# Attention in two passes: pass 1 of the next unit is issued between the key tiles of pass 2 of the current one

## The chip, the core and the metric

The kernel runs on one core of a Trainium2 chip. A core has a matrix engine (TensorE, PE in the profile; PEld is its weight load), a vector engine (VectorE, DVE), a scalar engine (ScalarE, ACT), GpSimd (POOL) and SyncE (SP); each works through its own queue in order, and they meet through semaphores. Transfers go through DMA queues that SP, ACT (here SPq and ACTq) and POOL issue. SBUF is the working memory; PSUM takes the results of matmuls and has 8 banks of 2 KiB per partition. The metric is the device time of one execution in microseconds (us).

## The reference

Two layers work on 2048 tokens of width 1024 and are mixed by a gate. The change is in layer A, softmax attention with 32 heads of 32:

```python
def _A_ref(x, wqkv, wo):
    qkv = (x @ wqkv).reshape(B, S, 3, H, Dh).transpose(2, 0, 3, 1, 4)
    q, k, v = (qkv[0], qkv[1], qkv[2])
    scale = Dh ** (-0.5)
    scores = jnp.einsum('bhqd,bhkd->bhqk', q, k) * scale
    p = _softmax(scores, axis=-1)
    o = jnp.einsum('bhqk,bhkd->bhqd', p, v)
    return o.transpose(0, 2, 1, 3).reshape(B, S, D) @ wo
...
g = _sigmoid((x * gate_w).sum(-1, keepdims=True))
return g * a + (1 - g) * b
```

Layer B (`b`) is a recurrence over 64 segments of 32 tokens; each needs the memory that the one before wrote.

## The kernel before

The program has three stages, one after the other: the projections of layer A (with the transposes of x and the gate), attention with its output projection (`phaseA_attn`), and the recurrence of layer B (`phase2_recurrence`), which adds A's part at the end. Only `phaseA_attn` is touched.

Attention runs over 4 query chunks (`qc`) of 512 queries and, in each, 8 groups (`g`) of 4 heads: 32 units. For a unit, four `KTm` tiles (a head's keys, 128 x 2048, other heads' rows zero) and four `Qaug` tiles (128 x 512 queries) are loaded from `ka_s` and `qa_s` by SP's and ACT's queues (L454, L455), into one of two sets of buffers, and POOL clears one row of each `Qaug` (L456). A unit has two passes:

- Pass 1 finds each query's largest score. For 4 heads, 4 query tiles and 4 key chunks, 64 in all, PE makes a score tile `sq`, 128 queries x 512 keys (L462), and DVE takes its maximum into `mp` (L464). Then DVE folds `mp` into `negm` (L466), 16 small transposes turn it into rows in `nr_ps` (L470), and ACT and DVE in turn (`ev`, L56 and L58) copy one row into each `Qaug` (L473). KTm has ones there, so pass 2 gets the maximum subtracted by its matmul.
- Pass 2 goes over 16 key tiles. In each, for every head, PE makes `st`, 128 keys x 512 queries (L479), and ACT takes the exponent into `p_sb` (L482); then a group of four matmuls per head adds its product with the values to `o_ps` (L486), whose last column is the sum. At the end DVE takes reciprocals, multiplies by the gate `gcol` and scales into `OA` (L493 to L499).

After 8 units the chunk is projected: for 4 query tiles, 8 transposes of `OA` into `trA` (L506), a copy `oat`, and 16 matmuls with `wo_sb` into `psA3` (L513), which are copied to `stageA` and stored (L516).

PSUM is shared out by pools: `pq` has 3 banks for everything tagged `sq` (`sq`, `nr_ps`, `trA`, `psA3`), `pt` 3 for `st`, `po` 2 for `o_ps`. The order on each engine is not that of the text: the framework's scheduler places instructions by priority (earlier in the text first) and by when buffers and inputs are free. So pass 1 of a unit already starts, in the order, during pass 2 of the unit before.

## Time and profile before

| | |
|---|---|
| median of 6 runs | 4604.24 us (4595.59 to 4608.38) |
| the profiled execution: its time, its span | 4595.59 us, 4593.8 us |
| busy share of the span: PE, DVE, ACT | 87%, 48%, 34% |
| first maximum of attention to its last `negm` | 249.63 us to 1945.43 us |
| mean granted clock of TensorE | 0.917 |

The span goes from the first to the last instruction of the profiled execution. Shares over the whole span mix stages: attention takes some 1755 us of it and the recurrence the last 2590 us, which keeps the DMA engines busy and DVE and ACT not. In attention the clock row of the profile stands at 7 to 8 tenths, in the recurrence at 9. A time in the rows below is counted from the span's start. A line such as L58 or L56 is the copy helper's; the tile names tell what was copied. Busy time of an engine that overlaps its own next instruction (the mean of one is then longer than the spacing) counts once.

### The profile page before, as it was taken

Reading aid. Unit: us, or ns where it says so; the run is one execution under the profiler, and the core shown is the slowest. Engines: PE = TensorE matmul, PEld = TensorE weight load, DVE = VectorE, ACT = ScalarE, POOL = GpSimd, SP = SyncE. Lnnn points to the kernel's source line nnn. Section 1 sums busy time; section 2 is a strip of 40 time slices with the busy share of each in tenths; the row PEclk is TensorE's granted clock in tenths of the full one; section 3 lists DMA queues with packets and bytes.
Section 4 is the critical chain, followed back from the end, with each engine's and each line's share of the span. In section 5 each row is a group of like instructions: output and inputs, shape, how many; then the busy total and the mean of one; then the engine's idle time right before and its main releaser. Section 6 shows DMA issues by size and latency. Waiting matters only on the chain.

```text
span 4593.8 us, 127170 instructions
## 1 busy us (share of the span) xinstructions
PE 4005.2 (87%) x57232; PEld 2042.9 (44%) x57476; DVE 2216.5 (48%) x3778; ACT 1576.4 (34%) x3049; POOL 285.5 (6%) x524
## 2 busy tenths in 40 slices
PE   6978889888898898859898888888888888888888
...
DMA packets 235026, 918.69 MB, mean 200 GB/s; under 512 B 23016, under 2 KB 39400, under 8 KB 158832
## 3 DMA queue, kind: packets, MB, share of 16 engines
...
q14 instruction: 96, 0.79, 0.1%
...
## 4 chain that ended last, share of the span: by engine, by line
PE 55%; ACT 14%; DVE 14%; DMA 12%; issue 4%; POOL 0%; ACTq 0%; SPq 0%; POOLq 0%; DVEq 0%
PE pjm L259 11%; PE wps L359 11%; DVE mp L464 11%; DMA wp<-in_B_Wk_dram 10%; PE pjx L259 9%; ACT p_sb L482 9%; PE st L479 6%; PE sq L462 4%; PE o_ps L486 3%; PE tr L282 2%; PE ps L402 2%; PE ops L340 1%; ACT QmT L56 1%; PE psA L513 1%; PE ops L343 1%
## 5 line engine op out<-in xcount | busy, mean ns | idle before, releaser
L464 DVE TENSOR_REDUCE mp<-sq 128x1 f32<-128x512 f32 x2048 | 1287.8, 683 | 171.7 <-PE sq L462 169.7
L482 ACT ACTIVATE p_sb<-st 128x512 bf16<-128x512 f32 x2048 | 1019.0, 722 | 46.8 <-PE st L479 44.0
L462 PE MATMUL sq<-KTm,Qaug 128*128 128x512 bf16 x2020 | 891.6, 448 | 111.4 <-DVE mp L464 73.3
L479 PE MATMUL st<-Qaug,KTm 128*128 128x512 bf16 x1856 | 705.9, 393 | 20.3 <-ACT Qaug L56 13.7
L486 PEld LDWEIGHTS <-p_sb 128*128 128x128 bf16 x8192 | 433.2, 97 | 478.3 <-ACT p_sb L482 298.8
L259 PEld LDWEIGHTS <-memT 128*32 128x32 bf16 x12288 | 360.3, 97 | 475.2 <-issue 178.1
L486 PE MATMUL o_ps<-V_A,p_sb 128*128 128x33 bf16 x8192 | 524.7, 180 | 20.3 <-ACT p_sb L482 13.9
L259 PEld LDWEIGHTS <-xs 128*32 128x32 bf16 x12288 | 386.5, 97 | 285.4 <-issue 5.9
L259 PE MATMUL pjm<-wp,memT 128*32 128x512 bf16 x4608 | 362.6, 382 | 104.9 <-DMA wp<-in_B_Wk_dram 103.5
L462 PEld LDWEIGHTS <-Qaug 128*128 128x128 bf16 x2048 | 196.9, 99 | 429.8 <-issue 402.2
L259 PE MATMUL pjx<-wp,xs 128*32 128x512 bf16 x4608 | 362.5, 381 | 0.2 <-issue 0.2
L359 PEld LDWEIGHTS <-oT 128*32 128x32 bf16 x8128 | 229.2, 103 | 254.2 <-issue 67.4
L359 PE MATMUL wps<-res_o,oT 128*32 128x512 bf16 x5080 | 338.6, 405 | 0.0
L370 DVE SCALAR_TENSOR_TENSOR bo<-wps,omg,apt 64x512 bf16<-64x512 f32 x64 | 48.4, 757 | 505.1 <-ACT memn L56 498.7
L58 DVE CAST tm_km<-pjm 128x512 bf16<-128x512 f32 x64 | 44.3, 692 | 489.7 <-PE pjm L259 489.7
L58 DVE CAST tm_qm<-pjm 128x512 bf16<-128x512 f32 x64 | 44.3, 692 | 454.4 <-PE pjm L259 454.4
L259 PE MATMUL pjm<-res_q,memT 128*32 128x512 bf16 x2560 | 198.4, 382 | 66.5 <-DVE memT L58 52.0
L56 ACT COPY Qaug<-nr_ps 1x512 bf16<-1x512 bf16 x64 | 37.0, 578 | 584.6 <-PE nr_ps L470 569.8
L359 PE MATMUL wps<-wp,oT 128*32 128x512 bf16 x3048 | 226.8, 419 | 1.5 <-DMA wp<-in_B_Wo_dram 1.1
L56 ACT CAST tm_qm<-pjm 128x512 bf16<-128x512 f32 x64 | 37.5, 586 | 538.3 <-PE pjm L259 498.3
L259 PE MATMUL pjx<-res_v,xs 128*32 128x512 bf16 x2560 | 207.1, 379 | 0.3 <-issue 0.3
L259 PE MATMUL pjm<-res_v,memT 128*32 128x512 bf16 x2560 | 207.0, 380 | 0.0
...
## 6 DMA issues: line engine op xcount, KB each, us to landing
...
```

The source lines that it names most:

```text
L56: self.nc.scalar.copy(out=out, in_=in_)
L58: self.nc.vector.tensor_copy(out=out, in_=in_)
L259: nc.tensor.matmul(ps[u][32 * j:32 * j + 32, :], lhsT=lhs_of[w](kt), rhs=piece[:, c * 512:(c + 1) * 512], start=(kt == kts[0] and first), ...
L282: nc.tensor.transpose(tr[:, hp, :], tm[key][:, hp // 4, (hp % 4) * 128:(hp % 4 + 1) * 128], ident[:])
L359: nc.tensor.matmul(wps[32 * cg:32 * cg + 32, :], lhsT=lhsT, rhs=piece[:, hh, c * 512:(c + 1) * 512], start=(gi == 0 and hh == 0), stop=(gi ...
L370: nc.vector.scalar_tensor_tensor(out=bo[64:128], in0=wps[64:128, :], scalar=omg[64:128, s:s + 1], in1=apt[64:128], op0=ALU.mult, op1=ALU.add)
L402: nc.tensor.matmul(ps[:], lhsT=w_sb[:, kt, which * D + g * 128:which * D + (g + 1) * 128], rhs=xT[:, kt, ch * CH:(ch + 1) * CH], start=(kt ...
L462: nc.tensor.matmul(sq[:], lhsT=Qaug[b][hh][:, qt * 128:(qt + 1) * 128], rhs=KTm[b][hh][:, kc * KC:(kc + 1) * KC], start=True, stop=True)
L464: nc.vector.tensor_reduce(out=mp[:, hh, qt, kc:kc + 1], in_=sq[:], op=ALU.max, axis=AX.X)
L479: nc.tensor.matmul(st[:], lhsT=KTm[b][hh][:, kt * 128:(kt + 1) * 128], rhs=Qaug[b][hh][:], start=True, stop=True)
L482: nc.scalar.activation(out=p_sb[:], in_=st[:], func=ACT.Exp, scale=scale)
L486: nc.tensor.matmul(o_ps[qt // 2][:, qt % 2, hh, :], lhsT=pts[hh][:, qt * 128:(qt + 1) * 128], rhs=V_A[:, kt, 4 * g + hh, :], start=(kt == ...
```

## The change

The pass over units is written as a pipeline by hand. The first unit's pass 1 runs alone; then, in every key tile of a unit's pass 2, a sixteenth of the next unit's pass 1 follows (`pass1_slice`), and after the last key tile the next unit's maxima are finished (`pass1_finish`). Besides:

- A score tile `sq` is two banks, 128 x 1024, filled by two matmuls, and one DVE reduction takes the maximum of both: 32 reductions a unit. `mp` has every second column unused and is filled with -3e38 by POOL first.
- The pools `pq` and `pt` have two buffers each (`pq` now two of two banks).
- The four rows of `Qaug` are all copied by ACT.
- `o_ps` is copied to SBUF by DVE (`o_sb`), the reciprocals and the gate are applied there, and ACT scales into `OA`, 16 instructions of 128 x 32 a unit, with the factor as an operand of one value per partition.
- In the projection, `psA3` is two banks and is copied at once.

```diff
@@ -429,8 +429,8 @@
     cp = ctx.enter_context(tc.tile_pool(name="a2c", bufs=1))
     wk = ctx.enter_context(tc.tile_pool(name="a2w", bufs=2))
     ptp = ctx.enter_context(tc.tile_pool(name="a2pt", bufs=8))
-    pq = ctx.enter_context(tc.tile_pool(name="a2psq", bufs=3, space=PSUM))
-    pt = ctx.enter_context(tc.tile_pool(name="a2pst", bufs=3, space=PSUM))
+    pq = ctx.enter_context(tc.tile_pool(name="a2psq", bufs=2, space=PSUM))
+    pt = ctx.enter_context(tc.tile_pool(name="a2pst", bufs=2, space=PSUM))
     po = ctx.enter_context(tc.tile_pool(name="a2pso", bufs=1, space=PSUM))
 
     ident = cp.tile([128, 128], BF16, name="identA")
...
+    units = [(qc, g) for qc in range(NQC) for g in range(8)]
+    NU = len(units)
+    state = {}
+
+    def load(u):
+        qc, g = units[u]
+        b = u % 2
+        for hh in range(4):
+            dq[hh % 2].dma_start(KTm[b][hh][32 * hh:32 * hh + 32, :], ka_s[g, 32 * hh:32 * hh + 32, :])
+            dq[(hh + 1) % 2].dma_start(Qaug[b][hh][:], qa_s[g, :, qc * QC:(qc + 1) * QC])
+            nc.gpsimd.memset(Qaug[b][hh][RS[hh]:RS[hh] + 1, :], 0.0)
+        mp = wk.tile([128, 4, NQT, NKC], FP32, name="mp")
+        if KCG > 1:
+            nc.gpsimd.memset(mp[:], -3.0e38)
+        state[u] = dict(mp=mp)
+
+    KCG = 2 if NKC % 2 == 0 else 1
+    p1_items = [(hh, qt, kc) for hh in range(4) for qt in range(NQT) for kc in range(0, NKC, KCG)]
+
+    def pass1_slice(u, i, n):
+        b = u % 2
+        mp = state[u]["mp"]
+        lo, hi = i * len(p1_items) // n, (i + 1) * len(p1_items) // n
+        for hh, qt, kc in p1_items[lo:hi]:
+            sq = pq.tile([128, 2, 512], FP32, name="sq", tag="sq")
+            for i in range(KCG):
+                nc.tensor.matmul(sq[:, i, 0:KC], lhsT=Qaug[b][hh][:, qt * 128:(qt + 1) * 128],
+                                 rhs=KTm[b][hh][:, (kc + i) * KC:(kc + i + 1) * KC], start=True, stop=True)
+            nc.vector.tensor_reduce(out=mp[:, hh, qt, kc:kc + 1], in_=sq[:, 0:KCG, 0:KC], op=ALU.max, axis=AX.XY)
+
+    def pass1_finish(u):
+        b = u % 2
+        negm = wk.tile([128, 4, NQT], BF16, name="negm")
+        nc.vector.tensor_reduce(out=negm[:], in_=state[u]["mp"][:], op=ALU.max, axis=AX.X, negate=True)
+        nr_ps = pq.tile([128, 2 * 1024], BF16, name="nr_ps", tag="sq")
+        for hh in range(4):
+            for qt in range(NQT):
+                nc.tensor.transpose(nr_ps[RS[hh]:RS[hh] + 1, qt * 128:(qt + 1) * 128],
+                                    negm[:, hh, qt:qt + 1], ident[:], tile_position=(0, RS[hh]))
+        for hh in range(4):
+            nc.scalar.copy(out=Qaug[b][hh][RS[hh]:RS[hh] + 1, :], in_=nr_ps[RS[hh]:RS[hh] + 1, 0:QC])
+
+    def pass2_iter(u, kt):
+        qc, g = units[u]
+        b = u % 2
+        if kt == 0:
+            state[u]["o_ps"] = [po.tile([128, 2, 4, DA + 1], FP32, name=f"o_ps{i}") for i in range((NQT + 1) // 2)]
+        o_ps = state[u]["o_ps"]
+        pts = []
+        for hh in range(4):
+            st = pt.tile([128, QC], FP32, name="st")
+            nc.tensor.matmul(st[:], lhsT=KTm[b][hh][:, kt * 128:(kt + 1) * 128], rhs=Qaug[b][hh][:],
+                             start=True, stop=True)
+            p_sb = ptp.tile([128, QC], BF16, name="p_sb")
+            nc.scalar.activation(out=p_sb[:], in_=st[:], func=ACT.Exp, scale=scale)
+            pts.append(p_sb)
+        for hh in range(4):
+            for qt in range(NQT):
+                nc.tensor.matmul(o_ps[qt // 2][:, qt % 2, hh, :], lhsT=pts[hh][:, qt * 128:(qt + 1) * 128],
+                                 rhs=V_A[:, kt, 4 * g + hh, :],
+                                 start=(kt == 0 and hh == 0 and qt % 2 == 0), stop=(kt == nkt - 1),
+                                 skip_group_check=True)
+
+    def finalize(u, OA):
+        qc, g = units[u]
+        for i, ops_ps in enumerate(state[u]["o_ps"]):
+            nq = min(2, NQT - 2 * i)
+            ops = wk.tile([128, 2, 4, DA + 1], FP32, name=f"o_sb{i}")
+            nc.vector.tensor_copy(out=ops[:, 0:nq], in_=ops_ps[:, 0:nq])
+            rs = wk.tile([128, 2, 4], FP32, name="rs")
+            nc.vector.reciprocal(rs[:, 0:nq, :], ops[:, 0:nq, :, DA])
+            gq = gcol[:, qc * NQT + 2 * i:qc * NQT + 2 * i + nq]
+            nc.vector.tensor_tensor(out=rs[:, 0:nq, :], in0=rs[:, 0:nq, :],
+                                    in1=gq.unsqueeze(2).to_broadcast([128, nq, 4]), op=ALU.mult)
+            for q2 in range(nq):
                 for hh in range(4):
...
+                    nc.scalar.activation(out=OA[:, 2 * i + q2, 4 * g + hh, :], in_=ops[:, q2, hh, 0:DA],
+                                         func=ACT.Copy, scale=rs[:, q2, hh:hh + 1])
+        del state[u]
+
+    def out_proj(qc, OA):
         for qt in range(NQT):
             tt = qc * NQT + qt
...
+            tr = pq.tile([128, 2 * KT, 128], BF16, name="trA", tag="sq")
             OAf = OA[:, qt].rearrange("p h d -> p (h d)")
             for kt in range(KT):
                 nc.tensor.transpose(tr[:, kt, :], OAf[:, kt * 128:(kt + 1) * 128], ident[:])
             oat = wk.tile([128, KT, 128], BF16, name="oat")
...
+            ev(oat[:], tr[:, 0:KT, :])
             stage = wk.tile([128, D], FP32, name="stageA")
+            ps = pq.tile([128, 2, 512], FP32, name="psA3", tag="sq")
             for c in range(2):
...
                 for kt in range(KT):
...
+                    nc.tensor.matmul(ps[:, c, :], lhsT=oat[:, kt, :], rhs=wo_sb[:, kt, c * 512:(c + 1) * 512],
                                      start=(kt == 0), stop=(kt == KT - 1))
...
+            ev(stage[:].rearrange("p (c f) -> p c f", c=2), ps[:])
             nc.gpsimd.dma_start(ap_s[tt * 128:(tt + 1) * 128, :], stage[:])
+
+    load(0)
+    pass1_slice(0, 0, 1)
+    pass1_finish(0)
+    OA = None
+    for u in range(NU):
+        qc, g = units[u]
+        if g == 0:
+            OA = wk.tile([128, NQT, HA, DA], BF16, name="OA")
+        if u + 1 < NU:
+            load(u + 1)
+        for kt in range(nkt):
+            pass2_iter(u, kt)
+            if u + 1 < NU:
+                pass1_slice(u + 1, kt, nkt)
+        if u + 1 < NU:
+            pass1_finish(u + 1)
+        finalize(u, OA)
+        if g == 7:
+            out_proj(qc, OA)
```

The scheduler decides what this makes of the queues. On DVE, at the end of a unit (`L493` to `L499` before and `L516` to `L520` now are the unit's last scaling steps), stood:

```order
L464 TENSOR_REDUCE mp<-sq 128x1 x43
L493 RECIPROCAL rs<-o_ps_4739 128x8
L493 RECIPROCAL rs<-o_ps_4740 128x8
L497 TENSOR_SCALAR rs<-rs,gcol 128x4 x2
L499 TENSOR_TENSOR OA<-o_ps_4739,rs 128x128 x2
L497 TENSOR_SCALAR rs<-rs,gcol 128x4 x2
L499 TENSOR_TENSOR OA<-o_ps_4740,rs 128x128 x2
L464 TENSOR_REDUCE mp<-sq 128x1 x18
L466 TENSOR_REDUCE negm<-mp 128x16
```

and now stands:

```order
L476 TENSOR_REDUCE mp<-sq 128x1 x32
L481 TENSOR_REDUCE negm<-mp 128x16
L516 COPY o_sb_7274<-o_ps_6609 128x264
L516 COPY o_sb_7287<-o_ps_6610 128x264
L518 RECIPROCAL rs<-o_sb_7274 128x8
L518 RECIPROCAL rs<-o_sb_7287 128x8
L520 TENSOR_TENSOR rs<-rs,gcol 128x8 x2
```

The 18 maxima that stood behind the end of the current unit stand ahead of it, and each is twice as long.

On ACT, between two units' exponents (`p_sb`), stood:

```order
L482 ACTIVATE p_sb<-st 128x512 x63
L455 DMA Qaug_0_1470<-qa_s 128x512
L454 DMA KTm_1_1463<-ka_s 32x2048
L455 DMA Qaug_2_1472<-qa_s 128x512
L454 DMA KTm_3_1465<-ka_s 32x2048
L56 COPY Qaug_0_1474<-nr_ps 1x512
L482 ACTIVATE p_sb<-st 128x512
L56 COPY Qaug_2_1476<-nr_ps 1x512
L482 ACTIVATE p_sb<-st 128x512 x63
```

and now stands:

```order
L502 ACTIVATE p_sb<-st 128x512 x3
L456 DMA KTm_1_1467<-ka_s 32x2048
L488 COPY Qaug_0_1470<-nr_ps 1x512
L488 COPY Qaug_1_1471<-nr_ps 1x512
L488 COPY Qaug_2_1472<-nr_ps 1x512
L488 COPY Qaug_3_1473<-nr_ps 1x512
L524 ACTIVATE OA<-o_sb_8809,rs 128x32 x8
L524 ACTIVATE OA<-o_sb_8822,rs 128x32 x8
L457 DMA Qaug_2_1476<-qa_s 128x512
L456 DMA KTm_3_1469<-ka_s 32x2048
L502 ACTIVATE p_sb<-st 128x512 x61
```

Four copies, sixteen scalings and two of the loads' issues moved in between the exponents of one unit and the next.

On PE, at the first score tile of the unit after next (its `Qaug` and `KTm` take the buffers of the unit just ending), stood, behind all the `o_ps` groups and the small transposes:

```order
L462 LDWEIGHTS Qaug1_0_1474
L462 MATMUL sq_6786<-KTm1_0_1466,Qaug1_0_1474 128x512
L462 LDWEIGHTS Qaug1_0_1474
L462 MATMUL sq_6789<-KTm1_0_1466,Qaug1_0_1474 128x512
L479 LDWEIGHTS KTm0_0_1462
L479 MATMUL st_6249<-Qaug0_0_1470,KTm0_0_1462 128x512
```

and now stands, at one such place:

```order
L474 LDWEIGHTS Qaug1_0_1474
L474 MATMUL sq_11703<-KTm1_0_1466,Qaug1_0_1474 128x512
L474 LDWEIGHTS Qaug1_0_1474
L474 MATMUL sq_11703<-KTm1_0_1466,Qaug1_0_1474 128x512
L506 LDWEIGHTS p_sb_11580
L506 MATMUL o_ps0_10964<-V_A_69,p_sb_11580 128x33
```

The pair moved ahead of the last `o_ps` group of the ending unit.

## Rows read from the trace of the kernel before

**Rows 1.** Costliest groups: line, engine, tiles | busy us, mean ns | idle before, releaser.
```profile
L464 DVE TENSOR_REDUCE mp<-sq 128x1 f32<-128x512 f32 x2048 | 1287.8, 683 | 171.7 <-PE sq L462 169.7
L482 ACT ACTIVATE p_sb<-st 128x512 bf16<-128x512 f32 x2048 | 1019.0, 722 | 46.8 <-PE st L479 44.0
```

**Rows 2.** Busy us of each engine in stretches of one unit, then clock and DMA.
```profile
core 0: us, PE busy (x) PEld busy (x) DVE busy (x) ACT busy (x) POOL busy (x), PEclk, DMA share, GB/s
923.00:957.60 34.60, 33.54 (x360) 17.67 (x366) 30.24 (x48) 32.43 (x66) 0.00 (x0) 0.95 0.03 8
957.60:970.10 12.50, 8.77 (x17) 1.54 (x15) 12.47 (x30) 0.00 (x0) 2.07 (x4) 0.63 0.25 65
970.10:971.60 1.50, 1.17 (x17) 0.62 (x19) 0.24 (x2) 0.50 (x1) 0.00 (x0) 0.50 0.00 0
```

**Rows 3.** Timeline of DVE: start us, duration us, instruction, xcount [idle before <-releaser].
```profile
249.63 38.35 DVE L464 TENSOR_REDUCE mp<-sq 128x1 f32<-128x512 f32 x64 [16.94 <-PE sq L462]
288.02 0.22 DVE L466 TENSOR_REDUCE negm<-mp 128x16 bf16<-128x64 f32 x1
...
629.09 0.22 DVE L466 TENSOR_REDUCE negm<-mp 128x16 bf16<-128x64 f32 x1
...
726.46 0.22 DVE L466 TENSOR_REDUCE negm<-mp 128x16 bf16<-128x64 f32 x1
...
921.40 0.22 DVE L466 TENSOR_REDUCE negm<-mp 128x16 bf16<-128x64 f32 x1
...
959.17 10.84 DVE L464 TENSOR_REDUCE mp<-sq 128x1 f32<-128x512 f32 x18
970.05 0.22 DVE L466 TENSOR_REDUCE negm<-mp 128x16 bf16<-128x64 f32 x1
...
1945.43 0.22 DVE L466 TENSOR_REDUCE negm<-mp 128x16 bf16<-128x64 f32 x1
...
1980.97 0.28 DVE L493 RECIPROCAL rs<-o_ps 128x8 f32<-128x8 f32 x2 [31.61 <-PE o_ps L486]
```

**Rows 4.** Timeline of ACT around one unit boundary (ACTq: its DMA issues).
```profile
927.06 29.55 ACT L482 ACTIVATE p_sb<-st 128x512 bf16<-128x512 f32 x60 [0.85 <-PE st L479]
956.10 0.34 ACTq L455 DMA_DIRECT2D Qaug<-qa_s  x1
956.36 0.74 ACT L482 ACTIVATE p_sb<-st 128x512 bf16<-128x512 f32 x1
...
971.10 0.58 ACT L56 COPY Qaug<-nr_ps 1x512 bf16<-1x512 bf16 x1 [14.01 <-PE nr_ps L470]
972.38 0.60 ACT L482 ACTIVATE p_sb<-st 128x512 bf16<-128x512 f32 x1 [0.70 <-PE st L479]
```

**Rows 5.** Timeline of PE and PEld: in the output projection, at a boundary, in pass 2.
```profile
673.66 3.63 PE L513 MATMUL psA<-wo_sb,oat 128*128 128x512 bf16 x16 [0.79 <-DVE oat L58]
...
971.73 0.61 PE L479 MATMUL st<-Qaug,KTm 128*128 128x512 bf16 x1 [0.24 <-ACT Qaug L56]
...
973.03 0.29 PEld L486 LDWEIGHTS <-p_sb 128*128 128x128 bf16 x4 [0.65 <-ACT p_sb L482]
...
979.73 0.38 PE L479 MATMUL st<-Qaug,KTm 128*128 128x512 bf16 x1
979.94 0.38 PE L462 MATMUL sq<-KTm,Qaug 128*128 128x512 bf16 x1
980.16 0.26 PE L486 MATMUL o_ps<-V_A,p_sb 128*128 128x33 bf16 x4
980.26 0.66 PE L479 MATMUL st<-Qaug,KTm 128*128 128x512 bf16 x2
```

**Rows 6.** Timeline of POOL at the same boundary.
```profile
959.23 1.09 POOL L456 MEMSET Qaug<- 1x512 bf16 x2 [45.79 <-DMA Qaug<-qa_s]
```

**Rows 7.** Groups of ACT by line and shape, whole span: names, shapes | busy us, mean ns | idle before.
```profile
L56 ACT CAST oT<-ops 128x512 bf16<-128x512 f32 x128 | 75.0, 586 | 62.7 <-PE ops L343 62.7
L56 ACT COPY KTt<-tr 128x256 bf16<-128x256 bf16 x64 | 23.8, 373 | 14.4 <-PE tr L282 14.4
```

**Rows 8.** Who waited for whom, 925 to 957 us: us in total, times, longest.
```profile
PEld L486 <- ACT p_sb L482: 8.3, 32, 0.5
```

More of the change, by code (lines that the diff above doesn't have):

```diff
@@ L501, in phaseA_attn @@
+    def out_proj(qc, OA):
         for qt in range(NQT):
             tt = qc * NQT + qt
-            tr = pq.tile([128, KT, 128], BF16, name="trA", tag="sq")
+            tr = pq.tile([128, 2 * KT, 128], BF16, name="trA", tag="sq")
             OAf = OA[:, qt].rearrange("p h d -> p (h d)")
@@ L507, in phaseA_attn @@
             oat = wk.tile([128, KT, 128], BF16, name="oat")
-            ev(oat[:], tr[:])
+            ev(oat[:], tr[:, 0:KT, :])
             stage = wk.tile([128, D], FP32, name="stageA")
+            ps = pq.tile([128, 2, 512], FP32, name="psA3", tag="sq")
             for c in range(2):
-                ps = pq.tile([128, 512], FP32, name="psA3", tag="sq")
                 for kt in range(KT):
-                    nc.tensor.matmul(ps[:], lhsT=oat[:, kt, :], rhs=wo_sb[:, kt, c * 512:(c + 1) * 512],
+                    nc.tensor.matmul(ps[:, c, :], lhsT=oat[:, kt, :], rhs=wo_sb[:, kt, c * 512:(c + 1) * 512],
                                      start=(kt == 0), stop=(kt == KT - 1))
-                ev(stage[:, c * 512:(c + 1) * 512], ps[:])
+            ev(stage[:].rearrange("p (c f) -> p c f", c=2), ps[:])
             nc.gpsimd.dma_start(ap_s[tt * 128:(tt + 1) * 128, :], stage[:])
+    load(0)
[17 more added lines that the diff above has]
+            out_proj(qc, OA)
 @with_exitstack
```

53 lines of the change are left out of this document (removed).

## The prediction

> **What bounds the kernel now.** I read the costliest groups first, then the busy times of three stretches inside one unit, then the timelines of VectorE (DVE), ScalarE (ACT) and TensorE (PE) at one unit boundary. The costliest rows are the maximum `mp<-sq` on DVE, 2048 x 0.683 us alone, and the exponent `p_sb<-st` on ACT, 2048 x 0.722 us alone [rows 1]. Set in a row they come faster: 64 maxima in 38.35 us, 0.60 us each [rows 3], and 60 exponents in 29.55 us, 0.4925 us each [rows 4]. One unit has 64 of each, so 38.4 us of DVE and 31.5 us of ACT.
>
> The units are already overlapped: a unit's `negm` follows the last one's after 48.7 us (629.09 - 288.02 over 7 intervals, or 970.05 - 921.40) [rows 3], well under the 70 us of both passes. The overlap is partial. For 34.6 us both passes run and all three engines are nearly full (PE 33.5, ACT 32.4, DVE 30.2); then 12.5 us in which ACT does nothing, DVE is full and the clock falls to 0.63 [rows 2], while 18 maxima are worked off in 10.84 us [rows 3]; then 1.5 us of hand-over. At the change of a query chunk there is no overlap: the interval is 726.46 - 629.09 = 97.4 us [rows 3], since `trA` and `psA3` take the same PSUM buffers as `sq` and come first. So attention is 38.35 + 28 x 48.7 + 3 x 97.4 + 35.5 (the last pass 2, 1945.43 to 1980.97) plus the last output projection. The recurrence behind it is untouched and I give it no change.
>
> **The change part by part.** *Fewer, longer maxima.* 32 reductions over 1024 elements take the place of 64 over 512. No row shows 1024. From 64 elements (0.22 us [rows 3]) to 512 (0.683 [rows 1]) an element costs (0.683 - 0.22)/448 = 1.03 ns, so the longer one comes every 0.60 + 0.53 = 1.13 us. Below that is 2 x 0.53 = 1.06 (no fixed cost), above it 2 x 0.60 = 1.20 (nothing saved). 32 x 1.13 = 36.2 us a unit, 2.2 less than before. DVE also keeps about 1.7 us for `negm`, two copies of `o_ps` (264 elements, some 0.35 us each by the same slope), reciprocals (0.28 for two [rows 3]) and products.
>
> *Pass 1 spread over all of pass 2.* In the order of the instructions nearly all 64 `sq` matmuls of the next unit stand inside the current pass 2, against 42 to 46 before. The 12.5 us stretch goes. What is late next is PE and the ring of `st`.
>
> *The ring of `st`, 3 to 2.* This is the dear edit. From an `st` matmul's start to its exponent is 0.65 us at half clock, of which the matmul is 0.61 [rows 4, 5], so 0.04 of it is signalling; at full clock the matmul is 0.38 [rows 5], so 0.42. The exponent alone takes 0.60 [rows 4], and PE starts 0.05 after its end (972.98 to 973.03 [rows 4, 5]). A buffer's round is 0.42 + 0.60 + 0.05 = 1.07 us; with two buffers an exponent can come every 0.535 at best, above the 0.4925 of now. PE adds to it, being one queue. A key tile has 4 `st`, 4 `sq` and 4 groups of four `o_ps` matmuls; matmuls of 512 come every 0.215, a group takes 0.10 [rows 5], and I count 0.12 with its signals. Walking the new order with st0 at 0: group 3 of the last tile 0.22, st1 0.34, two `sq` 0.55 and 0.77, st2 1.07 (it waits for exponent 0), group 0 1.29, st3 1.57 (waits for exponent 1), group 1 1.78, `sq` 1.90, group 2 2.14 (waits for exponent 2), `sq` 2.26, next st0 2.47. That is 0.62 us per exponent. A tile without the last `sq` comes to 0.57, and the order has 3 to 4 `sq` in most tiles. So 63 exponents take 33.7 (0.535) to 39.1 us (0.62); I take 0.59, nearest to the walk, 37.2 us.
>
> *The hand-over between units.* On ACT the four copies into `Qaug` (two stood on DVE) and 16 scalings into `OA` (four DVE products before) now stand between the last exponent of a unit and the first of the next, and every exponent queues behind them. A copy of 256 elements takes 0.373 and of 512 0.586 [rows 7], so 0.83 ns per element and 0.16 fixed: a scaling of 32 elements is about 0.19, and 0.09 if they overlap as the exponents do (0.60 to 0.4925). That makes 1.4 to 3.0 us; I take 3.0, since the copy's rows are the nearest. They wait for the last `o_ps` group, two DVE copies, reciprocals and products: about 1.5 us after the last exponent, time in which the four copies (0.58 each [rows 4]) fit. Then the loads: unit u+2 goes into the buffers of unit u, and its `Qaug` transfer cannot be issued before u's last `st`. In the trace it is issued at 956.10 and the POOL memset behind it ends near 959.75 [rows 4, 6], 2.65 us after the last exponent's end (957.10). Until now 10.84 us of maxima hid that. In the new order the `sq` that need this load stand on PE ahead of the next unit's first `st` in 16 of 30 units (in five even ahead of the last `o_ps` group), and before its third `st` stand 10 to 16 of them in 23 units, 4 in four, none at the chunk changes: five to eight maxima, of which PE can be two ahead, so 4 to 8 us after the load in which the third exponent can't start. That work is not lost to DVE, but ACT stands. From the last exponent to the next steady ones: 4.5 us at least (ACT's own work), 7.2 with the wait for the load, 10.5 where eight maxima go first; I take 7.8, between the last two and nearer to the lower, since some units have few. The two `KTm` transfers on ACT's queue also go behind copies or scalings there, but are needed only 16 `sq` later. The new memset of `mp` on POOL is short and needed only by the next unit's maxima.
>
> The ScalarE page of the Trainium skill ("ScalarE: Activation LUTs", section "What ACT_TABLE_LOAD costs", its last lines) says that a `[128,1]` operand, such as the scale here, adds about 93 ns to an ACTIVATE; by it, after the overlap that it also gives, a scaling is 0.21 us and an estimate of the sum would be 12 us higher. No row of this trace has such an operand.
>
> *A unit.* 37.2 + 7.8 = 45.0 us, with ends 33.7 + 4.5 = 38.2 and 39.1 + 10.5 = 49.6. DVE sets a floor: 36.2 + 1.7 + about 2.5 from `negm` to the next maximum, 40.4 us.
>
> *The change of a chunk.* The new order puts the four blocks of the projection (16 matmuls in 3.63 us [rows 5], 8 transposes) ahead of the next `sq`, with about two exponents between blocks. Pass 2 goes on slowly for some 17 us and pass 1 moves back by as much: 45 + 17 = 62 us instead of 97.4.
>
> *The sum.* First pass 1: 36.2 - 38.35 = -2. 28 ordinary intervals: 28 x (45.0 - 48.7) = -104. Three chunk changes: 3 x (62 - 97.4) = -106. Last pass 2, alone, with two buffers: about 38 for 35.5, and scalings ahead of the last projection 3, +5.5. Together -206. On the profiled execution (4595.6 us) that is 4389; the median of the runs is 8.6 us above it. I say **4392 us**. Each microsecond of the unit is worth 31 us.
>
> **The rivals.** *DVE becomes the bound.* If two buffers suffice, because ACT falls behind and catches up, the unit is 40.4 us and the time 4392 - 31 x 4.6 = 4249; with units up to 43 us it is 4330. For it: the maxima alone fill 36 us. Against it: the round of 1.07 us.
>
> *The ring and PE's queue stop each other.* A late exponent holds an `st` or a group, this holds the `sq` behind it, and DVE's answer then holds PE. A key tile of 2.5 to 2.65 us behind hand-overs of 8 to 9 us gives units of 47 to 51 us: 4454 to 4578. For it: PE already waits for `p_sb` in the present pass 2 with three buffers (8.3 us in 32 waits [rows 8]). The trace-analysis page of the Trainium skill ("Perfetto Trace Analysis", section "Identifying Performance Opportunities") says that a gap that repeats can mean too little PSUM for the next tile, by count of buffers or size of tiles; this trace agrees so far that with three `st` buffers ACT set 60 exponents without a gap.
>
> *The clock.* In the stretch paced by DVE it fell to 0.63 [rows 2], and `st` took 0.61 at 971.73 but 0.38 at 979.73 [rows 5]. If the new hand-over pulls it down for long, a tile's PE work goes from 2.2 to some 4.1 us. With 4 of 16 tiles at 1.2 GHz the unit is 45 + 7.6 = 52.6 us, just past the 51.8 us (45 + (4604 - 4392)/31) at which the gain ends; with 6 it is 56.4 us and the kernel takes 4745, slower than before. Against it: the mixed stretch ran at 0.95 with the same work [rows 2].
>
> That nothing is overlapped anew is ruled out for the ordinary units by the order; at the chunk changes pass 1 could still be held longer than I say, which the range covers.
>
> **How the numbers follow.** Forecast (units of 43 to 47 us, 4330 to 4454): 0.60. DVE bound: 0.15. Ring: 0.19. Clock: 0.04. The rest, 0.02, is no difference: within 0.2%, about what a measurement can tell here. Faster is then 0.94, slower 0.04. The range, 4270 to 4500, takes in the forecast, most of the DVE case and the lower half of the ring case, about 0.8.
>
> **What would show it.** `negm` spacing of 45 us, 62 at three places; two-bank maxima of about 1.2 us each alone; exponents about 0.59 apart with ACT idle on `st`, and PE waiting for `p_sb`; scalings of about 0.19 us; some 8 us between the units' steady exponents. Spacing near 40 with DVE full says the ring doesn't matter; spacing over 47 with ACT and DVE both idle says it matters more; a low clock inside pass 2 is the slower case.

## The result, and the profile after

| | before | after |
|---|---|---|
| median | 4602.53 us (16 runs, 4594.01 to 4608.38) | 4479.99 us (8 runs, 4477.07 to 4492.98) |
| the profiled execution, its span | 4595.59 us, 4593.8 us | 4468.53 us, 4466.8 us |
| mean granted clock of TensorE | 0.917 | 0.955 |

The ratio is 0.9738 (95% interval 0.9728 to 0.9749): faster, by about 122 us. The forecast was 4392 us, a gain of 212; the time lies in its range (4270 to 4500) but near the upper end, where the rival of the ring and PE's queue stood.

The time of the profiled execution splits by `negm` as the prediction's sum does. Before, 28 ordinary intervals have a mean of 48.74 us and the three at the chunk changes 97.56; after, 46.52 and 72.89. From the timeline of DVE in the changed kernel, at the places that answer to [rows 3] (columns: start, duration, engine, line, operation, tiles, shapes, count, idle time ahead and what ended it):

```profile
252.56 37.26 DVE L476 TENSOR_REDUCE mp<-sq 128x1 f32<-128x1024 f32 x32 [19.93 <-POOL mp L461]
289.85 0.22 DVE L481 TENSOR_REDUCE negm<-mp 128x16 bf16<-128x64 f32 x1
...
663.31 0.22 DVE L481 TENSOR_REDUCE negm<-mp 128x16 bf16<-128x64 f32 x1
...
736.87 0.21 DVE L481 TENSOR_REDUCE negm<-mp 128x16 bf16<-128x64 f32 x1
...
780.25 0.22 DVE L481 TENSOR_REDUCE negm<-mp 128x16 bf16<-128x64 f32 x1
...
825.34 0.22 DVE L481 TENSOR_REDUCE negm<-mp 128x16 bf16<-128x64 f32 x1
...
1810.99 0.22 DVE L481 TENSOR_REDUCE negm<-mp 128x16 bf16<-128x64 f32 x1
```

The first `negm` is 1.8 us later than before. Eight intervals follow to 663.31, 46.7 us each on average (43.5 to 54.3); the chunk change takes 736.87 - 663.31 = 73.6 us, the next ordinary ones 43.4 and 45.1. From the last `negm` to the end of the span are 2655.8 us, 7.4 more than before. So +1.8 + 28 x (46.52 - 48.74) + 3 x (72.89 - 97.56) + 7.4 = -127 us, the whole difference of the two spans.

The groups of instructions on ACT, the exponents answering to the one in [rows 1], and the scalings (count, busy time, mean ns of one, idle time ahead):

```profile
L502 ACT ACTIVATE p_sb<-st 128x512 bf16<-128x512 f32 x2048 | 1130.7, 595 | 169.7 <-PE st L499 132.5 <-PE sq L474 6.5 <-ACT p_sb L502 0.2
L524 ACT ACTIVATE OA<-o_sb,rs 128x32 bf16<-128x32 f32 x512 | 112.1, 305 | 28.9 <-DVE rs L520 28.9
```

The exponents now wait 132.5 us for `st`, 44.0 before [rows 1]: that is where to look for the missing gain. Besides the chunk changes, it sits at two places, inside pass 2 and at the hand-over. First one ordinary unit in three stretches, as in [rows 2] (busy time of PE, PEld, DVE, ACT and POOL, then the granted clock and the DMA share):

```profile
780.25:788.10 7.85, 5.56 (x41) 2.12 (x40) 6.16 (x11) 7.10 (x24) 1.77 (x5) 0.87 0.41 113
788.10:792.30 4.20, 3.32 (x11) 1.16 (x12) 3.71 (x5) 0.94 (x2) 0.45 (x1) 0.50 0.00 0
792.30:825.30 33.00, 31.79 (x323) 15.84 (x328) 30.16 (x25) 30.86 (x56) 0.00 (x0) 0.99 0.00 1
```

For 33 us all three engines are above nine tenths, at full clock. In 4.2 us before that ACT stands (0.94 us busy), PE does little but feed DVE's maxima, and the granted clock is 0.50, the lower of its two levels (1.2 and 2.4 GHz). The 12.5 us in which ACT did nothing [rows 2] have shrunk to this.

The hand-over itself, at the next boundary, on ACT, answering to [rows 4]:

```profile
826.97 1.79 ACT L502 ACTIVATE p_sb<-st 128x512 bf16<-128x512 f32 x3 [0.15 <-PE st L499]
828.79 2.38 ACT L488 COPY Qaug<-nr_ps 1x512 bf16<-1x512 bf16 x4
831.07 1.16 ACT L524 ACTIVATE OA<-o_sb,rs 128x32 bf16<-128x32 f32 x5
...
834.47 1.05 ACT L502 ACTIVATE p_sb<-st 128x512 bf16<-128x512 f32 x2
839.80 1.08 ACT L502 ACTIVATE p_sb<-st 128x512 bf16<-128x512 f32 x2 [4.28 <-PE st L499]
```

and at the same time on PE, answering to [rows 5]:

```profile
829.41 0.38 PE L499 MATMUL st<-Qaug,KTm 128*128 128x512 bf16 x1 [0.33 <-DMA KTm<-ka_s]
830.45 0.61 PE L474 MATMUL sq<-KTm,Qaug 128*128 128x512 bf16 x1 [0.66 <-POOL Qaug L458]
830.85 0.63 PE L499 MATMUL st<-Qaug,KTm 128*128 128x512 bf16 x1
831.71 1.06 PE L474 MATMUL sq<-KTm,Qaug 128*128 128x512 bf16 x2 [0.22 <-PE st L499]
...
834.43 0.59 PE L474 MATMUL sq<-KTm,Qaug 128*128 128x512 bf16 x2 [0.31 <-DVE mp L476]
...
838.95 0.59 PE L474 MATMUL sq<-KTm,Qaug 128*128 128x512 bf16 x2 [0.54 <-DVE mp L476]
839.38 0.38 PE L499 MATMUL st<-Qaug,KTm 128*128 128x512 bf16 x1
```

The last exponent ends at 828.76. Copies and scalings take ACT until 834.4, 5.7 us. Two exponents follow, whose `st` PE had made early. Then ACT waits 4.28 us, since PE's queue holds pairs of `sq` ahead of the third `st`, and each pair waits for a maximum (a pair every 1.13 us). The third `st` starts at 839.38 and its exponent at 839.80, 11 us after the last exponent's end. Over 24 ordinary boundaries (the chunk changes, the first after each and the last one left out) this third exponent starts 8.7 to 11.8 us after, 10.1 on average.

### The profile page after: what moved, and what is told of

It reads as the page before. It is cut to its first block, busy times and chain, and to the rows that moved or that the text cites. A ratio compares the mean times of both kernels' runs of the same rounds, so it can differ in the third digit from the quotient of the medians.

```text
span 4466.8 us, 126026 instructions
## 1 busy us (share of the span) xinstructions
PE 3865.8 (87%) x57226; PEld 2040.9 (46%) x57476; DVE 2111.4 (47%) x2554; ACT 1829.0 (41%) x3617; POOL 290.3 (6%) x556
## 4 chain that ended last, share of the span: by engine, by line
PE 59%; ACT 16%; DMA 13%; DVE 6%; issue 4%; POOL 1%; ACTq 0%; SPq 0%; POOLq 0%; DVEq 0%
PE pjm L259 12%; PE wps L359 11%; ACT p_sb L502 10%; DMA wp<-in_B_Wk_dram 10%; PE pjx L259 9%; PE st L499 6%; PE sq L474 6%; DVE mp L476 4%; PE o_ps L506 3%; PE tr L282 2%; PE ps L402 2%; PE ops L340 2%; ACT QmT L56 1%; PE ops L343 1%; PE psA L541 1%
## 5 line engine op out<-in xcount | busy, mean ns | idle before, releaser
L476 DVE TENSOR_REDUCE mp<-sq 128x1 f32<-128x1024 f32 x1024 | 1219.4, 1221 | 171.2 <-PE sq L474 81.3
L502 ACT ACTIVATE p_sb<-st 128x512 bf16<-128x512 f32 x2048 | 1130.7, 595 | 169.7 <-PE st L499 132.5
L474 PE MATMUL sq<-KTm,Qaug 128*128 128x512 bf16 x1965 | 703.9, 404 | 131.8 <-DVE mp L476 62.1
L499 PE MATMUL st<-Qaug,KTm 128*128 128x512 bf16 x1905 | 724.1, 385 | 38.8 <-ACT p_sb L502 22.0
L58 DVE CAST tm_km<-pjm 128x512 bf16<-128x512 f32 x64 | 44.3, 692 | 480.4 <-PE pjm L259 480.4
L58 DVE CAST tm_qm<-pjm 128x512 bf16<-128x512 f32 x64 | 44.3, 692 | 457.6 <-PE pjm L259 457.6
L56 ACT CAST memn<-wps 64x512 bf16<-64x512 f32 x63 | 36.5, 579 | 491.9 <-PE wps L359 491.9
L56 ACT CAST tm_km<-pjm 128x512 bf16<-128x512 f32 x64 | 37.5, 586 | 479.0 <-PE pjm L259 479.0
L499 PEld LDWEIGHTS <-KTm 128*128 128x128 bf16 x2048 | 189.6, 97 | 76.4 <-issue 27.3
```

The costliest lines, as they stand in the source:

```text
L56: self.nc.scalar.copy(out=out, in_=in_)
L58: self.nc.vector.tensor_copy(out=out, in_=in_)
L474: nc.tensor.matmul(sq[:, i, 0:KC], lhsT=Qaug[b][hh][:, qt * 128:(qt + 1) * 128], rhs=KTm[b][hh][:, (kc + i) * KC:(kc + i + 1) * KC], start ...
L476: nc.vector.tensor_reduce(out=mp[:, hh, qt, kc:kc + 1], in_=sq[:, 0:KCG, 0:KC], op=ALU.max, axis=AX.XY)
L499: nc.tensor.matmul(st[:], lhsT=KTm[b][hh][:, kt * 128:(kt + 1) * 128], rhs=Qaug[b][hh][:], start=True, stop=True)
L502: nc.scalar.activation(out=p_sb[:], in_=st[:], func=ACT.Exp, scale=scale)
```

## The experiments

The theory: in the changed kernel ACT's chain sets the unit (the ring of two `st` buffers inside pass 2, then copies, scalings and the wait for the third `st`), and DVE, which set the unit before, has slack. Its rivals: DVE's maxima set it, or PE's queue does, and the ring is only where the wait shows. Ratios are against the kernel before on the same chip; "unit" and "chunk" are the mean `negm` intervals of the profiled execution. The kernels with a one-bank `o_ps` leave out the softmax sums, those with half maxima half of the scores that a maximum is taken of. A gain in us is taken between two medians on one chip, or as the difference of two gains over the kernel before.

| kernel | median us | ratio, interval | unit | chunk |
|---|---|---|---|---|
| after | 4479.99 | 0.9738, 0.9728 to 0.9749 | 46.5 | 72.9 |
| one-bank `o_ps`, two `st` (control) | 4477.57 | 0.9734, 0.9708 to 0.9760 | 46.4 | 73.1 |
| one-bank `o_ps`, three `st` | 4406.27 | 0.9580, 0.9542 to 0.9618 | 44.5 | 69.6 |
| scaling on DVE | 4385.39 | 0.9538, 0.9512 to 0.9563 | 44.3 | 66.2 |
| one-bank `o_ps`, three `st` and scaling on DVE | 4374.94 | 0.9515, 0.9497 to 0.9532 | 44.1 | 66.5 |
| the same, half of each maximum | 4269.12 | 0.9281, 0.9260 to 0.9301 | 41.4 | 60.2 |
| after, half of each maximum | 4460.38 | 0.9699, 0.9677 to 0.9721 | 46.3 | 72.8 |
| three sets of loads | 4455.63 | 0.9691, 0.9665 to 0.9718 | 45.3 | 72.7 |
| all loads on SP's queue | 4430.78 | 0.9641, 0.9619 to 0.9664 | 45.4 | 69.0 |
| projection spread over units | 4468.08 | 0.9718, 0.9696 to 0.9740 | 46 / 52 | none |
| old shares of PSUM, one-bank `sq` | 4409.71 | 0.9590, 0.9574 to 0.9606 | 44.5 | 71.7 |
| the new order of units alone | 4442.92 | 0.9661, 0.9642 to 0.9680 | 46.2 | 67.5 |
| kernel before with the new shares | 4579.69 | 0.9962, 0.9947 to 0.9977 | 47.6 | 101.5 |

**The ring of `st`.** Three `st` buffers with two-bank `sq` need a ninth bank; `o_ps` gave it up.

```diff
-    pt = ctx.enter_context(tc.tile_pool(name="a2pst", bufs=2, space=PSUM))
+    pt = ctx.enter_context(tc.tile_pool(name="a2pst", bufs=3, space=PSUM))
...
-            state[u]["o_ps"] = [po.tile([128, 2, 4, DA + 1], FP32, ...) ...]
+            o_all = po.tile([128, 2, 2, 4, DA], FP32, name="o_ps0")
+            state[u]["o_ps"] = [o_all[:, i] for i in range(2)]
```

> The changed kernel with three `st` buffers, two-bank `sq` kept. The bank for it comes from `o_ps`, which holds 32 columns per head instead of 33 and lies in one bank; the softmax sums are left out (the reciprocal is taken of a value column). Ring theory (two buffers set an exponent every 0.585 to 0.63 us): with three, exponents come every 0.50 to 0.53 us, 63 of them save 3.5 to 6 us a unit, and the order puts 8 instead of 10 to 16 `sq` ahead of the third `st`, another 1 to 3 us. Units of 39.5 to 42.5 us, DVE becoming the next limit, 4270 to 4370 us. Rival (DVE's maxima or PE's queue set the unit, the ring is only where the wait shows): within 15 us of the run that has this `o_ps` and two buffers.

Elsewhere `o_ps` and `o_sb` lose the column of sums, and the reciprocal is taken of a value column. The control has all of this but the first two lines:

> Control for the three-buffer run: the same one-bank `o_ps` without the sum column (softmax sums left out), but two `st` buffers as in the changed kernel. Both theories: 32 columns for 33 change nothing that can be measured, 4465 to 4495 us, units of 46 to 47 us. The order has 16 `sq` ahead of the third `st` in more units than the changed kernel (five of eight instead of two); if that count sets the hand-over, it is up to 1.5 us a unit, 30 to 45 us, slower than the changed kernel.

The control takes the time of the changed kernel, so the slimmer `o_ps` and the order that comes with it (more units with 16 `sq` ahead, and none of 54 us) are together worth nothing. The third `st` is worth 71 us: between the two expectations. ACT's timeline with three shows why:

```profile
814.42 9.97 ACT L503 ACTIVATE p_sb<-st 128x512 bf16<-128x512 f32 x20
...
842.01 0.59 ACT L503 ACTIVATE p_sb<-st 128x512 bf16<-128x512 f32 x1
...
846.89 0.32 ACT L525 ACTIVATE OA<-o_sb,rs 128x32 bf16<-128x32 f32 x1 [4.30 <-DVE rs L521]
847.24 2.38 ACT L488 COPY Qaug<-nr_ps 1x512 bf16<-1x512 bf16 x4
```

Twenty exponents stand in a row, 0.49 us apart, as in the kernel before [rows 4]. With two buffers (the changed kernel) the exponents come in two patterns:

```profile
500.91 2.15 ACT L502 ACTIVATE p_sb<-st 128x512 bf16<-128x512 f32 x4 [0.37 <-PE st L499]
503.42 2.15 ACT L502 ACTIVATE p_sb<-st 128x512 bf16<-128x512 f32 x4 [0.37 <-PE st L499]
...
661.71 3.47 ACT L502 ACTIVATE p_sb<-st 128x512 bf16<-128x512 f32 x6
665.48 1.34 ACT L502 ACTIVATE p_sb<-st 128x512 bf16<-128x512 f32 x2 [0.30 <-PE st L499]
```

Four exponents and a wait of 0.37 for `st` make 2.52 us a key tile (0.63 each; the walk in the prediction gave 2.47); elsewhere they are 0.57 to 0.59 apart. So in such stretches the ring costs what the forecast said, 0.1 us per exponent. Over a whole pass the third buffer gives back less: from the fifth exponent of a unit to the last, the mean spacing falls from 0.594 us in the control to 0.534, some 3.5 us a unit, where 0.49 would give 6. PE's records fill all of that stretch (1.00, for 0.98 in the control), so the rest is probably PE's own work, which no run takes away. The hand-over does not gain: the fifth exponent starts 12.3 us after the last one of the unit before (11.9 in the control), for ACT is done 4.3 us before DVE's last steps let it go on (846.89). By `negm`, 2 us a unit remain. A second limit of some 44 us lies right behind the first.

**Scaling on DVE.** The final scaling as before, from `o_ps`, with no `o_sb`:

```diff
-            ops = wk.tile([128, 2, 4, DA + 1], FP32, name=f"o_sb{i}")
-            nc.vector.tensor_copy(out=ops[:, 0:nq], in_=ops_ps[:, 0:nq])
+            ops = ops_ps
...
-                    nc.scalar.activation(out=OA[...], in_=ops[:, q2, hh, 0:DA], func=ACT.Copy, scale=rs[:, q2, hh:hh + 1])
...
+                nc.vector.tensor_tensor(out=OA[:, qt, 4 * g:4 * g + 4, :], in0=ops[:, q2, :, 0:DA], ...)
```

> The changed kernel with the final scaling as it was before: four DVE products straight from `o_ps`, no `o_sb` copies, no 16 scalings on ACT. Theory (the hand-over is ACT's queue and the `sq` that stand ahead of the third `st`): 3.4 us of ACT go, and the order now has 4 `sq` ahead of the third `st` in place of 10 to 16, so two maxima instead of five to eight: hand-over from about 10 to 4 to 6 us, 4 to 6 us a unit, 4290 to 4360 us. If only the scalings' own time counts: 31 x 3.4 = 105 us, 4375. Rival (PE and DVE set the unit; ACT stands in the hand-over anyway): 4465 to 4490, since DVE has about 0.5 us more work a unit.

It came out at 4385.39 us, 2.2 us a unit and 6.7 a chunk change better than the changed kernel: less than the theory's 4290 to 4360, near the 4375 of the scalings' own time. It is the fastest kernel here that leaves nothing out. ACT's hand-over:

```profile
841.34 0.59 ACT L502 ACTIVATE p_sb<-st 128x512 bf16<-128x512 f32 x1
...
844.00 2.38 ACT L488 COPY Qaug<-nr_ps 1x512 bf16<-1x512 bf16 x4 [2.07 <-PE nr_ps L485]
846.28 2.19 ACT L502 ACTIVATE p_sb<-st 128x512 bf16<-128x512 f32 x4
```

Four exponents follow the copies without a gap: 4 `sq` stand between the second `st` and the third, where 10 to 16 stood ahead of it. The third exponent starts 6.7 us after the last one on average (10.1 in the changed kernel). From the fifth exponent on they come every 0.60 us in both kernels, so this edit changes the hand-over and leaves the ring. Since ACT now waits 2.07 us for `negm`'s transposes, DVE is near the path here as well.

**Both together, and a lighter DVE.**

> Three `st` buffers (with `o_ps` of 32 columns in one bank, softmax sums left out) and the final scaling on DVE as before, both edits together. Each alone gave units of 44.3 to 44.5 us (2.1 and 2.2 us less than the changed kernel). If they are separate terms on one path: 42 to 42.5 us, about 4310 us; the DVE floor is 40.4, 4260. Rival (a common limit of 44.3 us, DVE's maxima with PE's order of the `sq`): units of 44 us, 4370 to 4385 us, and only the chunk changes gain.

The rival came true: 44.1 us, and 4375. The two edits don't add up. DVE and ACT at one boundary of this kernel:

```profile
822.42 16.98 DVE L476 TENSOR_REDUCE mp<-sq 128x1 f32<-128x1024 f32 x14 [0.30 <-PE sq L474]
```

```profile
834.42 0.59 ACT L503 ACTIVATE p_sb<-st 128x512 bf16<-128x512 f32 x1
...
840.49 2.38 ACT L488 COPY Qaug<-nr_ps 1x512 bf16<-1x512 bf16 x4 [5.47 <-POOL mp L461]
```

ACT has finished at 835.0 and idles 5.47 us; the wait is put down to POOL, which had long been done, and in that time DVE works off its last maxima, without a pause, until 839.4. (16.98 - 1.22)/13 = 1.21 us is their spacing. To see whether the maxima are the limit, both this kernel and the changed one were given maxima over half of their columns:

```diff
-            nc.vector.tensor_reduce(out=mp[:, hh, qt, kc:kc + 1], in_=sq[:, 0:KCG, 0:KC], op=ALU.max, axis=AX.XY)
+            nc.vector.tensor_reduce(out=mp[:, hh, qt, kc:kc + 1], in_=sq[:, 0:KCG, 0:KC // 2], op=ALU.max, axis=AX.XY)
```

> Three `st` buffers and scaling on DVE (softmax sums left out, as in the run that had both), and each maximum over half of its columns (half of the maxima left out). There units were 44.1 us with ACT done 5.5 us ahead of the next unit's copies. If DVE's maxima set that: units fall to 39 to 41.5 us, where PE (about 40 us of work a unit) is the next limit, 4220 to 4300 us. Rival (PE's queue or the hand-over sets 44 us): units of 43 to 44.5 us, 4345 to 4380 us.

> The changed kernel with each maximum over half the columns of both its banks (512 elements instead of 1024; the other half of the maxima is left out), all else alike: DVE's maxima cost 0.6 instead of 1.2 us, PE and ACT do the same work. If the ring of two `st` and the hand-over on ACT set the changed kernel's unit (46.5 us): exponents stay at 0.58 to 0.63 us, only the wait for maxima in the hand-over shrinks (the order has 17 `sq` ahead of the third `st`, nine short maxima), units of 44 to 46.5 us, 4400 to 4480 us. Rival (DVE's maxima set it): units of 40 to 42 us, 4270 to 4340 us.

With three buffers and scaling on DVE the unit falls to 41.4 us: DVE's maxima were its limit. In the changed kernel the same saving brings 12 us, no more than the first pass 1 saves by itself (its `negm` comes 14.8 us earlier), and the unit stays at 46.3. (The lighter maxima alter the order too; the first units of a chunk vary from 35 to 52 us, the others take 47 to 48.) ACT and PE of the changed kernel with half maxima:

```profile
817.07 1.05 ACT L502 ACTIVATE p_sb<-st 128x512 bf16<-128x512 f32 x2
822.62 28.79 ACT L502 ACTIVATE p_sb<-st 128x512 bf16<-128x512 f32 x50 [4.49 <-PE st L499]
```

```profile
815.07 6.11 PE L474 MATMUL sq<-KTm,Qaug 128*128 128x512 bf16 x14 [2.10 <-POOL Qaug L458]
```

Fifty exponents in 28.79 us are 0.575 us apart though DVE has time to spare: inside the pass DVE does not set the pace. A wait of 4.5 us stands in the hand-over again, but for another reason: the 14 `sq` come 0.42 us apart ((6.11 - 0.61)/13), at a granted clock of 0.50 (815.0 to 820.5). PE at its lower level took the place of DVE's maxima there, so this run does not show what the hand-over would be without them at full clock.

**The loads.** Three sets of `KTm` and `Qaug` let a load start early:

```diff
-    KTm = [[cp.tile([128, S], BF16, ...) for hh in range(4)] for b in range(2)]
+    KTm = [[cp.tile([128, S], BF16, ...) for hh in range(4)] for b in range(3)]
...
-        b = u % 2
+        b = u % 3
```

> The changed kernel with three sets of `KTm` and `Qaug` in place of two, so that the load of the unit after next no longer waits for the current unit's last `st`. Theory (load wait is a part of the hand-over): PE's waits for the memset row of `Qaug` (32.7 us in 18 waits between 300 and 1850 us) vanish, and the order has 10 `sq` ahead of the third `st` where it had up to 16: 1 to 3 us a unit, 4390 to 4450 us. Rival (the wait for the load lies beside the copies and scalings and costs nothing): 4470 to 4485.

With two sets, but all loads issued by SP:

```diff
-            dq[hh % 2].dma_start(KTm[b][hh][32 * hh:32 * hh + 32, :], ...)
-            dq[(hh + 1) % 2].dma_start(Qaug[b][hh][:], ...)
+            nc.sync.dma_start(KTm[b][hh][32 * hh:32 * hh + 32, :], ...)
+            nc.sync.dma_start(Qaug[b][hh][:], ...)
```

> The changed kernel with all loads of `KTm` and `Qaug` issued on SP's queue, none on ACT's, where they stand behind the copies and scalings of the hand-over. Theory (the first `sq` of the next unit wait for a load that ACT issues late; 5.2 us in the units of 54 us): the 54 us units fall to 46 to 48, others by 0 to 1 us, and the order has at most 10 `sq` ahead of the third `st`: units of 45 to 45.8 us, 4435 to 4460 us, about what three sets of buffers gave (4456). Rival (SP's one queue issues eight loads no earlier): 4475 to 4490 us.

Against the changed kernel both gain, 21 and 42 us, the second without a byte more memory. Three sets lose some of their gain at the start: the third set has to be filled too, the first `sq` waits 32.3 us for POOL in place of 21.3, and the first `negm` comes 11 us later. In the changed kernel ACT issues half of the loads from between the copies and scalings. In its four intervals of 54 us PE waited 4.7 to 5.4 us for that, as here

```profile
484.27 0.61 PE L474 MATMUL sq<-KTm,Qaug 128*128 128x512 bf16 x1 [5.17 <-POOL Qaug L458]
```

where the `Qaug` transfer was issued by ACT at 480.68, behind four copies and the first scalings. No price of this wait shows in the exponents: an interval of 54 is followed by one of 43 to 45; from third exponent to third exponent, the unit that ends in such a wait and the next take 95.0 us together, two other ordinary ones 95.2; and the control, which has none of them, is no faster. With all loads on SP's queue the units are even (43.5 to 46.7 us, no more of 54), and the third exponent starts 1.4 us after the first in place of 3.4:

```profile
816.32 1.05 ACT L502 ACTIVATE p_sb<-st 128x512 bf16<-128x512 f32 x2
817.93 1.14 ACT L502 ACTIVATE p_sb<-st 128x512 bf16<-128x512 f32 x2 [0.57 <-PE st L499]
819.62 0.60 ACT L502 ACTIVATE p_sb<-st 128x512 bf16<-128x512 f32 x1 [0.54 <-PE st L499]
```

So the gain lies in the hand-over of every unit. That the load is earlier and that at most 10 `sq` stand ahead of the third `st` come together here; how much each brings was not separated.

**The chunk change.** The projection taken apart, one query tile in each of four units of the next chunk:

```diff
             if u + 1 < NU:
                 pass1_slice(u + 1, kt, nkt)
+            if kt == 7 and u >= 8 and 1 <= g <= NQT:
+                out_proj(qc - 1, OAs[qc - 1], [g - 1])
```

> The changed kernel with the output projection of a chunk not in one piece at the chunk change but one query tile in each of the units 1 to 4 of the next chunk (the last chunk as before). In the changed kernel a chunk interval is 72.9 us against 46.5, 26.4 us more; PE's own work in it is 4 x 4.3 us = 17 us at full clock. If that work is the price wherever it stands, 3 x (26.4 - 17) = 28 us come back: 4440 to 4455 us. If it hides in PE's gaps (13 per cent of an ordinary unit, 6 us), up to 79 us: 4400. Rival (the blocks hold `sq` and `st` of the middle of a pass as badly as at its end): 4475 to 4500.

There is no long interval left, but every unit with a block takes 50.6 to 53.0 us against 43 to 47 for most units without one (four take 53 to 54, where PE waits 4.7 us for a late load as above): some 5 to 6 us a block, four blocks a chunk, nearly the 26.4 us that the piece cost. The interval of the ratio overlaps that of the changed kernel, so no gain is shown. A block in the changed kernel (PE, at the first chunk change):

```profile
671.25 0.23 PE L534 MATMUL trA<-identA,OA 128*128 128x128 bf16 x1 [1.69 <-ACT OA L524]
674.68 6.33 PE L541 MATMUL psA<-wo_sb,oat 128*128 128x512 bf16 x16 [3.20 <-ACT oat L56]
680.85 0.61 PE L534 MATMUL trA<-identA,OA 128*128 128x128 bf16 x8
...
682.56 3.63 PE L541 MATMUL psA<-wo_sb,oat 128*128 128x512 bf16 x15 [0.48 <-ACT oat L56]
...
687.80 3.63 PE L541 MATMUL psA<-wo_sb,oat 128*128 128x512 bf16 x16 [0.53 <-ACT oat L56]
...
696.49 0.59 PE L474 MATMUL sq<-KTm,Qaug 128*128 128x512 bf16 x2
```

Blocks follow each other after 687.80 - 682.56 = 5.24 us, and the first is dearer: it waits for ACT's scalings and for `oat` (4.9 us in two waits), and its matmuls run at half clock (6.33 for 3.63).

**What the parts are worth.** The new order of the units with everything else as in the kernel before, but for the `Qaug` copies and the preset of `mp` (three one-bank `sq`, three `st`, scaling on DVE), the same with the scaling on ACT, and the old order with the new shares:

```diff
-    pq = ctx.enter_context(tc.tile_pool(name="a2psq", bufs=2, space=PSUM))
-    pt = ctx.enter_context(tc.tile_pool(name="a2pst", bufs=2, space=PSUM))
+    pq = ctx.enter_context(tc.tile_pool(name="a2psq", bufs=3, space=PSUM))
+    pt = ctx.enter_context(tc.tile_pool(name="a2pst", bufs=3, space=PSUM))
...
-    KCG = 2 if NKC % 2 == 0 else 1
+    KCG = 1
```

The tiles in `pq`, those of the projection too, are one bank again.

> The changed order of the work with the PSUM shares of the kernel before: 64 one-bank maxima, three `sq`, three `st`; copies and scalings of the hand-over on ACT as in the changed kernel. If the ring of two `st` is the dear edit (three gave 2.3 us a unit with two-bank maxima): exponents come every 0.50 us, DVE needs 38.4 us of maxima and about 5 us around the hand-over, units of 43.5 to 45 us, 4375 to 4430 us: the new shares then cost more than the longer maxima bring. Rival (64 short maxima on a DVE that is already the next limit): units of 46.5 to 48 us, 4480 to 4530 us.

> The new order of the units alone: PSUM shares, one-bank maxima and final scaling on DVE as in the kernel before; only the copies into `Qaug` stay on ACT and `mp` is preset on POOL as in the changed kernel. If DVE's maxima and what stands with them set a common limit of 44.1 to 44.5 us, which three kernels have shown: units of 44 us, chunk changes of 66 us (as with the scaling on DVE) instead of 71.7, 4370 to 4390 us, so the new shares and the scalings on ACT together cost some 100 us of what the order brings. Rival (the scalings on ACT are hidden with three `st`): 4405 to 4415 us, as with one-bank maxima alone.

> The kernel before, in its old order of units, with only the new PSUM shares: two `sq` of two banks, 32 maxima over 1024 elements, two `st`, and the projection's two-bank tiles. Theory (two `st` buffers cost about 0.09 us an exponent; the longer maxima save 2 us of DVE): the stretch with both passes grows from 34.6 to 37 to 39 us, the DVE stretch shrinks by about 1 to 2: units of 50 to 52 us, 4640 to 4700 us. Rival (DVE sets the unit of the kernel before, the shares are neutral or a gain): 4540 to 4600 us.

The gain against the kernel before, in us, new order throughout:

| | scaling on ACT | scaling on DVE |
|---|---|---|
| old shares (one-bank `sq`, three `st`) | 188 | 152 |
| new shares (two-bank `sq`, two `st`) | 122 | 213 |

So the new shares cost 66 us with the scaling on ACT, as the ring theory says. The rest contradicts my expectations. With the old shares the scaling on DVE loses 36 us instead of gaining some; the run fell outside both ranges. Its unit ends on DVE:

```profile
807.79 9.11 DVE L476 TENSOR_REDUCE mp<-sq 128x1 f32<-128x512 f32 x15 [0.24 <-PE sq L474]
...
834.10 1.89 DVE L476 TENSOR_REDUCE mp<-sq 128x1 f32<-128x512 f32 x3 [0.33 <-PE sq L474]
```

```profile
817.99 2.38 ACT L488 COPY Qaug<-nr_ps 1x512 bf16<-1x512 bf16 x4 [8.78 <-PE nr_ps L485]
```

In the middle of a pass DVE gets three `sq` per key tile of 2.2 us and waits for the next (second line); so 15 are left to be worked off in a row at the end of a unit (first line, the boundary before), while ACT idles 8.8 us. In the trace 51 of the 64 `sq` start before the last `st` of a unit here, 56 with the scaling on ACT, 62 with the new shares and scaling on DVE: the scheduler lets the place of the scaling move the `sq`. That this placement makes the 36 us fits the rows but was not tried by itself.

And in the old order the new shares gain 18 us, where I had expected a loss (the rival named this time). ACT's wait there says why two `st` cost nothing:

```profile
912.20 0.58 ACT L56 COPY Qaug<-nr_ps 1x512 bf16<-1x512 bf16 x1 [7.19 <-PE nr_ps L471]
```

ACT still idles 7.19 us here at the end of the unit, for 14.01 in the old kernel [rows 4]. The exponents come every 0.61 us for 0.50, some 6.6 us a unit, and that went into time that ACT had to spare.

## Why the prediction was right in direction, and where it missed

The terms of the sum fall short in the same direction: units 42 us, chunk changes 33, start and end 6. That the range held the time owes something to its upper end, which was drawn for the ring's rival. The sum itself gives 4398 us (4604 - 206) and not the 4392 that was stated.

- **The 12.5 us stretch goes:** right. Both passes now fill 33 us of a unit, with 4 us of DVE alone.
- **The ring, 0.59 us per exponent:** right in size. Patterns of 0.57 to 0.63; from the third exponent on 0.607 on average over 24 units. That is 1.1 us a unit above the value taken. But only 0.06 of the 0.1 us above the old spacing comes back with a third buffer. The trace-analysis page of the Trainium skill ("Perfetto Trace Analysis", section "Identifying Performance Opportunities") says that a gap that repeats can mean too little PSUM for the next tile. The runs agree in part: from the sixth exponent of a unit on, ACT's idle time falls from 2.5 to 1.7 us a unit with a third buffer, and some gaps of 0.37 us stay.
- **The hand-over, 7.8 us:** too low. The third exponent starts 10.1 us after the last one's end; less two exponents (1.05) that is 9.0, within the ends 4.5 to 10.5 but 1.2 above the value taken. ACT's own part is 5.7 and not 4.5: I let the four copies lie inside the 1.5 us of waiting for the scalings, where four of 0.58 do not fit; they take 2.38 us, the scalings stand behind them, and 16 of those take 3.49 us. A scaling is 0.305 us alone and 0.21 in a row; the rows of before had given 0.19. The ScalarE page of the Trainium skill ("ScalarE: Activation LUTs", section "What ACT_TABLE_LOAD costs") says that an operand of one value per partition adds about 93 ns; an estimate by its figures is 0.31 alone and 0.21 in a row, and this trace agrees. Then come 10 to 16 `sq`, also near the upper end. And a load that ACT itself issued late makes PE wait some 5 us in four units, though no price of it shows: I had named the queue for `KTm`, where the `Qaug` transfers, which are needed first, stand in it as well.
- **The unit, 45.0 us:** 46.5, by the hand-over (+1.2) and the ring (+1.1); the first unit after a chunk change is shorter (43.4 to 44.9). 28 x 1.5 = 42 of the missing us.
- **The chunk change, 62 us:** 72.9, the worst term; 3 x 10.9 = 33 of the missing us. I counted 17 us for four blocks, PE's own work. A block takes 5.2 us, because each waits for its `oat` and lets two `st` through, and the first adds 4.9 us of waiting and 2.7 at half clock. Together that is 28 us, for the 26.4 that a chunk change takes beyond a unit.
- **First pass and end:** +1.8 and +7.4 where I had -2 and +5.5. The maxima of pass 1 alone come every (37.26 - 1.22)/31 = 1.16 us, and POOL's preset of `mp` and the loads delay their start by 3 us (252.56 against 249.63 [rows 3]).
- **The DVE rival:** not the limit inside the pass (in the hand-over its maxima do pace the `sq` ahead of the third `st`), and its floor of 40.4 us was too low. The maxima come every 1.16 to 1.21 us beside other work, 1.13 only in the hand-over, and DVE waits for a `sq` in between. Four kernels stand at 44.1 to 44.5 us. That DVE's maxima set this is shown for one of them, by the half maxima, and argued for the others. So with the longer maxima even three `st` buffers gave some 4375 to 4410, not 4249.
- **The ring and PE's queue together:** it named this time (4454 to 4578) but gave units of 47 to 51 us and nothing for the chunk change. A unit of 46.5 was inside my forecast; the total went past it by the chunk changes.
- **The clock:** not the slower case. Between the first and the last `negm` it stands at the lower level for 163 us in all, 520 before: 3.4 to 10.2 us at most hand-overs, where PE goes at the pace of DVE's maxima or waits, and 6.8 us at a chunk change, where the first block pays 2.7.
